# Attention with global tokens and an expert layer: q and k transposed on TensorE, or cast through DRAM and transposed by DMA

## The chip, the cores and the metric

The kernel runs on one core of one Trainium2 chip. The metric is the device time of one execution in microseconds (us). Executions of one kernel mostly agree within about 0.5%. "Faster" or "slower" needs a difference of 2% that is clear of noise.

Engines: PE is TensorE's matmul, PEld its weight load, DVE is VectorE, ACT is ScalarE, POOL is GpSimd, SP is SyncE. On this kernel SP only issues DMAs. POOL also casts, and its DMAs go through another queue than SP's.

## The reference, cut to what matters

There are 8 batches of 8 heads. Each head has 512 local and 32 global tokens of 64 elements. Local tokens attend to the globals and to local tokens within a distance of 32; globals attend to all.

```python
k_all = concat([k_g, k_l]); v_all = concat([v_g, v_l])
out_g = softmax(scale * q_g @ k_all.T) @ v_all
s_l   = concat([scale * q_l @ k_g.T, where(|i-j| <= 32, scale * q_l @ k_l.T, -1e9)])
out_l = softmax(s_l) @ v_all
x = concat([out_g, out_l]) as (4352 tokens, 512)
h = x @ w_in                       # 512 -> 2048
out = (h * clip(h + 3, 0, 6) / 6) @ w_out
```

## The kernel before

The work of a batch is four pairs of heads. The kernel's score matmuls take q and k with the 64 elements of each head on the partitions: `kT` and `qT`, 128 partitions for two heads. DRAM holds them token by token. From the third batch on the kernel before does this:

```python
# SP loads q and k as fp32, tokens on the partitions        (load_qk)
nc.sync.dma_start(out=nat[b][0][i][:, kb], in_=(k_l, q_l)[i][b, :, kb*P:(kb+1)*P, :].rearrange(...))
# POOL casts a pair's part to fp16                           (cast_rows)
copies[i](out=r[m][i], in_=f[i][:, :, 2*m:2*m+2])

def emit_globals(b):               # once a batch: 8 matmuls, one DVE cast, two ACT casts
    ...
    nc.tensor.matmul(out=gT[:, i, m], lhsT=gz[b % 2][:, i, 2*m:2*m+2]..., rhs=ident[:, 0:Sg])
    nc.vector.tensor_copy(out=kgT[b % 2], in_=gT[:, 0])
    for e in range(2):
        nc.scalar.copy(out=qgz[b % 2][r, :, e*Sg:(e+1)*Sg], in_=gT[r, 1])

def emit_T(p):                     # once a pair: 8 transposes, 4 DVE copies, 1 ACT copy
    psT = ps_tile("psT", FP16)     # one of 7 PSUM buffers that everything shares
    for t, ps in zip(nat[b][1][m], src):
        for j in range(NT):
            nc.tensor.matmul(out=ps[:, j*P:(j+1)*P], lhsT=t[:, j]..., rhs=ident, is_transpose=True)
    nc.vector.tensor_copy(out=kT[:, <two places for the globals>], in_=kgT[b % 2][:, m:m+1]...)
    for k0, k1, c0 in SEG:         # three segments
        nc.vector.tensor_copy(out=kT[:, c0:c0 + k1 - k0], in_=src[0][:, k0:k1])
    nc.scalar.copy(out=qT, in_=src[1])

def emit_QK(p):                    # scores: psG for the globals, four psS buffers
    ...
    for t in range(2):
        pss = [ps_tile(f"psS{e}") for e in range(2)]
        ...                        # psS matmuls of this half
        for e in range(2):
            nc.scalar.activation(out=E[:, e, t], in_=pss[e][:, 0:SW], func=EXP, scale=qk_scale)
            nc.vector.tensor_tensor(out=E[:, e, t], in0=E[:, e, t], in1=mask[:, t], op=mult)
        ...

for p in range(NPAIR):             # software pipeline over pairs
    ...
    emit_T(p + 2)
    cast_rows(b + 1, m, pool)
    M(1)                           # M(n): n units of the previous batch's expert layer
    emit_QK(p + 1)
    M(4)
    emit_AV(p, lambda: M(1))
    M(2)
```

A unit of M is four 128x512 matmuls, into `psH` (first layer; ACT and DVE then make `t` and `gt` of it) or into `po` (second layer; DVE copies it to `ot`). The order on PE, ACT and DVE is set by a scheduler that starts from this program order; the order on POOL and SP is that of the program.

The softmax here doesn't subtract the row's maximum and nothing guards it: scores larger than these inputs give would overflow.

Of the kernel before, what the change touches and what calls it, by code (L numbers as in the profile page):

```python
# [9 lines left out]
FP32 = mybir.dt.float32  # L10
FP16 = mybir.dt.float16
# [3 lines left out]
def kernel(  # L15
# [12 lines left out]
    nc = tc.nc  # L28
    ctx.enter_context(tc.manual_schedule(engines={mybir.EngineType.Pool, mybir.EngineType.SP}))
    P = 128  # L30
    B, H, Sl, D = q_l.shape
    Sg = q_g.shape[2]
    S = Sg + Sl
    dm, dff = moe_w_in.shape
    NM = H // 2
    NC = dff // P
    NT = Sl // P
# [9 lines left out]
    SEG = [(0, 128, 0), (128, 288, 160), (288, 512, 352)]  # L47
    KC = [0, 128, 192, 320, 448]
    GC = [128, 320]
    KW = Sl + 2 * Sg  # L50
# [14 lines left out]
    natp = ctx.enter_context(tc.tile_pool(name="natp", bufs=2))  # L65
    wrk = ctx.enter_context(tc.tile_pool(name="wrk", bufs=2))
    moew = ctx.enter_context(tc.tile_pool(name="moew", bufs=4))
    psp = ctx.enter_context(tc.tile_pool(name="psp", bufs=7, space=bass.MemoryType.PSUM))
    psg = ctx.enter_context(tc.tile_pool(name="psg", bufs=1, space=bass.MemoryType.PSUM))

    def ps_tile(name, dtype=FP32):
        return psp.tile([P, 2048 // (4 if dtype == FP32 else 2)], dtype, tag="ps", name=name)
# [3 lines left out]
    def const(name, shape, dtype=FP16):  # L76
        return constp.tile(shape, dtype, tag=name, name=name)

    ident = const("ident", [P, P])
    kgT = [const(f"kgT{i}", [P, NM, Sg]) for i in range(2)]  # L80
# [10 lines left out]



    NR = 2

    def f_rows(t):
        return t.rearrange("p (kb h d) -> p kb h d", kb=NT, h=H)

    def load_runs(b, i, h0, nh):
        nc.gpsimd.dma_start(  # L100
# [8 lines left out]

    nat = {}  # L110

    def new_nat(b):
        if b < NR:
            f = [natp.tile([P, H, NT, D], FP16, tag=t, name=t, bufs=1) for t in ("k16", "q16")]
        else:
            f = [f_rows(natp.tile([P, NT * H * D], FP32, tag=t, name=t, bufs=1))
                 for t in ("f0", "f1")]
        nat[b] = (f, {})

    def load_qk(b):  # L120
        new_nat(b)
        for i in range(2):
            if b < NR:
                load_runs(b, i, 0, H)
                continue
            for kb in range(NT):
                nc.sync.dma_start(
                    out=nat[b][0][i][:, kb],
                    in_=(k_l, q_l)[i][b, :, kb * P:(kb + 1) * P, :].rearrange("h s d -> s h d"))


    def load_g(b, t=None):
        for i, src in enumerate((k_g, q_g)):
            (nc.gpsimd if t is None else nc.sync).dma_start(
                out=gz[b % 2][0:Sg, i] if t is None else t[:, i],
                in_=src[b].rearrange("h s d -> s h d"))

    def cast_rows(b, m, copies):
        f, r = nat[b]
        r[m] = [natp.tile([P, NT, 2, D], FP16, tag=f"{t}{m}", name=f"{t}{m}") for t in ("kr", "qr")]  # L140
        for i in range(2):
            copies[i](out=r[m][i],
                      in_=(f[i][:, 2 * m:2 * m + 2].rearrange("p h j d -> p j h d")
                           if b < NR else f[i][:, :, 2 * m:2 * m + 2]))

    def load_v(b):
        for c, r0, r1, src in v_parts(b, 0, H):
# [8 lines left out]
    def load_vf(b, h0, nh):  # L156
        for c, r0, r1, src in v_parts(b, h0, nh):
            nc.sync.dma_start(out=vf[b][r0:r1, c, h0:h0 + nh], in_=src)
# [4 lines left out]

    first = (nc.vector.tensor_copy, nc.scalar.copy)
    pool = (nc.gpsimd.tensor_copy, nc.gpsimd.tensor_copy)
    new_nat(0)
    new_vf(0)
    for i in range(2):
        load_runs(0, i, 0, 2)
# [33 lines left out]
    def emit_globals(b):  # L203
        psT = ps_tile("psGT")
        gT = psT[:, 0:2 * NM * Sg].rearrange("d (i m s) -> d i m s", i=2, m=NM)
        for i in range(2):
            for m in range(NM):
                nc.tensor.matmul(out=gT[:, i, m],
                                 lhsT=gz[b % 2][:, i, 2 * m:2 * m + 2].rearrange("s h d -> s (h d)"),
                                 rhs=ident[:, 0:Sg])  # L210
        nc.vector.tensor_copy(out=kgT[b % 2], in_=gT[:, 0])
        for e in range(2):
            r = slice(e * D, (e + 1) * D)
            nc.scalar.copy(out=qgz[b % 2][r, :, e * Sg:(e + 1) * Sg], in_=gT[r, 1])

    st = {}

    def emit_T(p):
        b, m = divmod(p, NM)
        kT = wrk.tile([P, KW], FP16, tag="kT", name="kT", bufs=4)  # L220
        qT = wrk.tile([P, Sl], FP16, tag="qT", name="qT", bufs=4)
        if b < NR:
            src = [ps_tile("psT") for _ in range(2)]
        else:
            psT = ps_tile("psT", FP16)
            src = [psT[:, i * Sl:(i + 1) * Sl] for i in range(2)]
        for t, ps in zip(nat[b][1][m], src):
            for j in range(NT):
                lhs = t[:, j].rearrange("p h d -> p (h d)")
                if b < NR:  # L230
                    nc.tensor.matmul(out=ps.rearrange("d (p j) -> d j p", j=NT)[:, j],
                                     lhsT=lhs, rhs=ident)
                else:
                    nc.tensor.matmul(out=ps[:, j * P:(j + 1) * P], lhsT=lhs, rhs=ident,  # L234
                                     is_transpose=True)
        nc.vector.tensor_copy(
            out=kT[:, GC[0]:GC[0] + 2 * (GC[1] - GC[0])].rearrange("d (i s) -> d i s", i=2)[:, :, 0:Sg],
            in_=kgT[b % 2][:, m:m + 1].to_broadcast([P, 2, Sg]))
        for k0, k1, c0 in SEG:
            nc.vector.tensor_copy(out=kT[:, c0:c0 + k1 - k0], in_=src[0][:, k0:k1])  # L240
        nc.scalar.copy(out=qT, in_=src[1])  # L241
        st[p] = dict(qT=qT, kT=kT)

    def emit_QK(p):
        b, m = divmod(p, NM)
        s = st[p]
        qT, kT = s["qT"], s["kT"]
        E = wrk.tile([P, 2, 2, SW], FP16, tag="E", name="E", bufs=3)
        Eg = wrk.tile([P, NCH, 2 * Sg], FP16, tag="Eg", name="Eg", bufs=3)
        s["E"], s["Eg"] = E, Eg  # L250
        psG = ps_tile("psG")
        for c in range(NCH):
            nc.tensor.matmul(out=psG[:, c * 2 * Sg:(c + 1) * 2 * Sg],  # L253
                             lhsT=kT[:, KC[c]:KC[c] + P], rhs=qgz[b % 2][:, m])
        for t in range(2):
            pss = [ps_tile(f"psS{e}") for e in range(2)]
            for c in range(NCH):
                if SC[c][0] != t:
                    continue
                c0, (_, _, q0, nq) = SC[c][1], CH[c]  # L260
                for e in range(2):
                    r = slice(e * D, (e + 1) * D)
                    nc.tensor.matmul(out=pss[e][:, c0:c0 + nq], lhsT=kT[r, KC[c]:KC[c] + P],  # L263
                                     rhs=qT[r, q0:q0 + nq])
            if t == 0:
                nc.scalar.activation(out=Eg, in_=psG[:, 0:NCH * 2 * Sg], func=EXP, scale=qk_scale)  # L266
# [3 lines that stand above are left out]
            if t == 0:  # L270
                nc.vector.tensor_tensor(out=Eg[:, 2:4], in0=Eg[:, 2:4], in1=maskg, op=mult)
# [116 lines left out]
    cast_vf(0, 3)  # L388
    new_vf(1)
    load_vf(1, 0, H)  # L390
    nc.vector.memset(vn[1][:, :, :, D:P], 1.0)
    for i in range(NC // 4):
        load_w_out(i)
# [4 lines left out]
    for p in range(NPAIR):  # L398
        b, m = divmod(p, NM)
        if m == 0 and b >= 1 and b + 1 < B:  # L400
            load_g(b + 1)
            load_v(b + 1)
        if p == NM:
            M(2)
            emit_globals(1)
            emit_T(p)
            M(1)
            emit_T(p + 1)
            M(1)
            emit_QK(p)  # L410
            M(1)
            load_qk(2)
        if m == 2 and 1 <= b < B - 1:
            emit_globals(b + 1)
        if p + 2 < NPAIR and p not in (NM - 2, NM - 1):
            emit_T(p + 2)
        if 1 <= b < B - 1:
            cast_rows(b + 1, m, pool)
            if m == NM - 1 and b + 2 < B:
                load_qk(b + 2)  # L420
        M(1)
        if p + 1 < NPAIR and p != NM - 1:
            emit_QK(p + 1)
        M(4)
        emit_AV(p, lambda: M(1))
        if m == NM - 1:
            M(len(units))
            units += moe_units(
                lambda mm, b=b: xts[b][mm], Sl,
                [[(0, P, b * S + Sg + t * P)] for t in range(NT)])  # L430
        else:
            M(2)
# [35 lines left out]
```

## Time and profile before

368.63 us, median of 3 runs (367.38 to 369.09).

| reading | before |
|---|---|
| span of the profiled execution | 366.0 us |
| PE busy | 91% |
| DVE, ACT busy | 68%, 68% |
| one batch in the steady part | 39.73 us |

The page's parts 1 and 2: busy time of PE, then the span in 40 slices, each digit the busy share of its slice in tenths.

```profile
span 366.0 us, 6783 instructions
...
PE 332.0 (91%) x2560; PEld 184.6 (50%) x2560; DVE 248.1 (68%) x577; ACT 247.0 (68%) x477; POOL 92.0 (25%) x144
...
PE   2575799998999999999999999999999999999994
...
ACT  2597399559975698559964897569855995274070
...
DMA  9999999259404990099107920397001000100202
...
```

PE is nearly full from the sixth slice on. ACT swings between nearly full (attention with the expert first layer) and half empty (with the second layer). The DMA row has zeros and ones in a good part of the steady slices. So there is idle DMA time to which work could be moved.

The windows view gives the steady state. The edges are the starts of the `xg` operations on DVE (the first of two a batch), which end each batch's attention. Columns: window, its length, then busy us and number of instructions of each engine.

```profile
...
core 0: us, PE busy (x) PEld busy (x) DVE busy (x) ACT busy (x) POOL busy (x), PEclk, DMA share, GB/s
123.91:163.64 39.73, 38.43 (x308) 20.82 (x308) 28.31 (x67) 29.53 (x57) 11.00 (x18) 1.00 0.60 93
163.64:203.38 39.74, 38.44 (x308) 20.86 (x308) 28.35 (x68) 29.52 (x57) 11.12 (x18) 1.00 0.68 104
...
```

What the transposes cost on PE, and how PE waits afterwards, is in the timeline of PE, in one pair of the fourth batch (start, duration, line, operation, count; in brackets idle time and who ended it):

```profile
...
132.69 0.39 PE L234 MATMUL psT<-ident,kr_1697 128*128 128x128 f16 x4
132.91 0.39 PE L234 MATMUL psT<-ident,qr_1698 128*128 128x128 f16 x4
...
134.81 0.29 PE L263 MATMUL psS_2037<-qT,kT 64*128 64x320 f16 x1 [0.19 <-DVE gt L330]
135.41 0.29 PE L263 MATMUL psS_2038<-qT,kT 64*128 64x320 f16 x1 [0.31 <-DVE gt L330]
...
```

Four transposes start every 0.22 us, so a pair's eight take 0.44 us of the stream, though each is shown with a longer duration (they are pipelined). The later psS matmuls wait twice for a PSUM buffer that DVE must empty. The timeline of ACT at the same place:

```profile
...
135.10 0.57 ACT L268 ACTIVATE E<-psS_2023 128x480 f16<-128x480 f32 x1
135.85 0.59 ACT L241 COPY qT<-psT 128x512 f16<-128x512 f16 x1 [0.18 <-DVE kT L240]
136.34 0.58 ACT L268 ACTIVATE E<-psS_2024 128x480 f16<-128x480 f32 x1
...
```

The qT copy stands between the first and the second E. It takes 0.49 us of ACT's stream, after 0.18 us of idle time in which it waits for DVE, and so puts off the three E operations that empty psS.

### The profile page before, as it was taken

The numbers are of one execution on the slowest core, as the hardware profiler recorded it, in microseconds if no ns is written. First come the engines' busy times: TensorE is split into PE (matmuls) and PEld (weight loads), VectorE is DVE, ScalarE is ACT, GpSimd is POOL, SyncE is SP. The second block draws the span as 40 slices with busy tenths as digits, with TensorE's granted clock in tenths as the row PEclk, the third lists the DMA queues.
The fourth block names the chain that finished last, engine by engine and source line by source line (L and its number), as shares of the span: only waits on it lengthen the run. The fifth ranks groups of instructions, "written<-read, shape, count | busy, mean of one in ns | idle before, by whom it ended". The sixth has DMA issues, their size and how long they took to land.

```text
span 366.0 us, 6783 instructions
## 1 busy us (share of the span) xinstructions
PE 332.0 (91%) x2560; PEld 184.6 (50%) x2560; DVE 248.1 (68%) x577; ACT 247.0 (68%) x477; POOL 92.0 (25%) x144
## 2 busy tenths in 40 slices
PE   2575799998999999999999999999999999999994
PEld 1553455565455555555555545555555544544471
DVE  7774698558875588558855888558855884485171
ACT  2597399559975698559964897569855995274070
POOL 7561581507400650044300830064000000000000
PEclk9996699999999999999999999999999999999998
DMA  9999999259404990099107920397001000100202
GB/s 149 214 196 184 200 210 160 36 140 211 47 3 111 206 107 2 29 201 189 9 31 152 226 18 2 108 209 102 3 30 57 30 1 30 57 30 0 86 31 57
DMA packets 109713, 35.38 MB, mean 97 GB/s; under 512 B 97136, under 2 KB 105328, under 8 KB 109680
## 3 DMA queue, kind: packets, MB, share of 16 engines
q0 software_dynamic: 43648, 10.69, 30.0%
q1 hardware_dynamic: 66032, 24.26, 29.9%
q8 instruction: 20, 0.33, 0.4%
q14 instruction: 13, 0.11, 0.1%
HBM read 36.70 MB, written 8.91 MB: 125 GB/s over the span
## 4 chain that ended last, share of the span: by engine, by line
PE 43%; ACT 29%; DVE 12%; DMA 7%; issue 5%; POOL 2%; DVEq 0%; ACTq 0%; POOLq 0%
PE po L339 28%; PE psH L324 7%; ACT E L268 7%; ACT Ln L300 5%; DMA gz_82<-in_q_g_dram 5%; DVE gt L330 4%; PE pav L296 4%; ACT Rc L303 3%; ACT qT L241 2%; DMA q_98<-in_q_l_dram 2%; DVE kT L240 1%; PE psT L234 1%; PE pg L298 1%; ACT Eg L266 1%; ACT Lg L311 1%
## 5 line engine op out<-in xcount | busy, mean ns | idle before, releaser
L339 PEld LDWEIGHTS <-gt 128*128 128x128 f16 x544 | 49.5, 97 | 54.1 <-issue 2.5
L300 ACT ACTIVATE Ln<-pav 64x512 f32<-64x512 f32 x64 | 38.0, 593 | 42.1 <-PE pav L296 36.4
L269 DVE TENSOR_TENSOR E<-E,mask 128x480 f16<-128x480 f16 x128 | 50.6, 410 | 9.6 <-ACT E L268 6.6
L343 DVE COPY ot<-po 128x512 f32<-128x512 f32 x34 | 23.5, 691 | 25.4 <-PE po L339 24.4
L339 PE MATMUL po<-wout_93,gt 128*128 128x512 f16 x136 | 35.0, 379 | 0.0
L339 PE MATMUL po<-wout_92,gt 128*128 128x512 f16 x136 | 34.9, 379 | 0.0
L339 PE MATMUL po<-wout_95,gt 128*128 128x512 f16 x136 | 34.9, 379 | 0.0
L339 PE MATMUL po<-wout_94,gt 128*128 128x512 f16 x136 | 34.9, 378 | 0.0
L148 POOL DMA_DIRECT2D vn_87<-in_v_l_dram x15 | 12.6, 850 | 67.6 <-PE pg L298 53.5
L148 POOL DMA_DIRECT2D vn_86<-in_v_l_dram x15 | 12.8, 864 | 49.0 <-PE pg L298 49.0
L266 ACT ACTIVATE Eg<-psG 128x320 f16<-128x320 f32 x32 | 13.9, 436 | 15.0 <-PE psG L253 14.9
L296 PE MATMUL pav<-E,vn_86 128*128 128x160 f16 (+3 forms) x160 | 21.5, 251 | 2.2 <-ACT Eg L266 1.2
L263 PEld LDWEIGHTS <-kT 64*128 64x128 f16 x320 | 12.8, 95 | 18.1 <-issue 13.8
L296 PE MATMUL pav<-E,vn_87 128*128 128x160 f16 (+3 forms) x160 | 21.3, 244 | 0.0
L324 PEld LDWEIGHTS <-win_88 128*128 128x128 f16 x144 | 14.0, 103 | 13.3 <-issue 2.0
L303 ACT ACTIVATE Rc<-Ln 128x512 f32<-128x512 f32 x32 | 20.0, 626 | 0.7
L324 PEld LDWEIGHTS <-win_90 128*128 128x128 f16 x144 | 13.3, 98 | 13.1 <-issue 1.2
L324 PEld LDWEIGHTS <-win_89 128*128 128x128 f16 x144 | 13.2, 98 | 12.5 <-issue 0.6
L324 PEld LDWEIGHTS <-win_91 128*128 128x128 f16 x144 | 13.1, 98 | 12.2 <-issue 0.2
L296 PEld LDWEIGHTS <-vn_86 128*128 128x128 f16 x160 | 14.9, 99 | 7.4 <-issue 3.1
L298 PE MATMUL pg<-Eg,vn_87 128*128 128x32 f16 x160 | 18.6, 178 | 0.0
L296 PEld LDWEIGHTS <-vn_87 128*128 128x128 f16 x160 | 14.9, 97 | 5.2
(967 smaller groups left out, 847.8 us busy)
## 6 DMA issues: line engine op xcount, KB each, us to landing
out_dram<-ot SPq DMA_DIRECT2D x32, 256.0 KB, 2.1
vn_86<-in_v_l_dram POOLq DMA_DIRECT2D x9, 128.0 KB, 6.8
vn_87<-in_v_l_dram POOLq DMA_DIRECT2D x9, 128.0 KB, 6.2
f_679<-in_k_l_dram SPq DMA_DIRECT2D x4, 256.0 KB, 5.8
f_680<-in_q_l_dram SPq DMA_DIRECT2D x4, 256.0 KB, 7.9
f_1135<-in_k_l_dram SPq DMA_DIRECT2D x4, 256.0 KB, 4.3
f_1136<-in_q_l_dram SPq DMA_DIRECT2D x4, 256.0 KB, 5.6
f_1701<-in_k_l_dram SPq DMA_DIRECT2D x4, 256.0 KB, 4.4
```

What stands on the lines that cost most here:

```text
L148: nc.gpsimd.dma_start(out=vn[b % NV][r0:r1, c, :, 0:D], in_=src)
L266: nc.scalar.activation(out=Eg, in_=psG[:, 0:NCH * 2 * Sg], func=EXP, scale=qk_scale)
L268: nc.scalar.activation(out=E[:, e, t], in_=pss[e][:, 0:SW], func=EXP, scale=qk_scale)
L269: nc.vector.tensor_tensor(out=E[:, e, t], in0=E[:, e, t], in1=mask[:, t], op=mult)
L296: nc.tensor.matmul(out=pav[:, q0:q0 + nq], lhsT=lhs, rhs=E[:, e, t, c0:c0 + nq], start=(i == 0), stop=(i == NCH - 1), skip_group_check=True)
L298: nc.tensor.matmul(out=pg[:, m, e], lhsT=lhs, rhs=Eg[:, c, e * Sg:(e + 1) * Sg], start=(i == 0), stop=(i == NCH - 1), skip_group_check=True)
L300: nc.scalar.activation(out=Ln[e * D:(e + 1) * D], in_=pav[D:P, 0:Sl], func=LN)
L303: nc.scalar.activation(out=Rc, in_=Ln, func=EXP, scale=-1.0)
L324: nc.tensor.matmul(out=ps[:, 0:n], lhsT=w_in_t[c // 4][:, m, (c % 4) * P:(c % 4 + 1) * P], rhs=rhs(m), start=(m == 0), stop=(m == NM - 1))
L330: nc.vector.scalar_tensor_tensor(out=gts[c][:, 0:n], in0=t1[:, 0:n], scalar=1.0, in1=ps[:, 0:n], op0=amin, op1=mult)
L339: nc.tensor.matmul(out=po[t][:, 0:dm], lhsT=gts[c][:, t * P:(t + 1) * P], rhs=w_out_t[c // 4][:, c % 4], start=(c == 0), stop=(c == NC - 1))
L343: nc.vector.tensor_copy(out=ot, in_=po[t][:, 0:dm])
```

## The change

The intent is to take the transposes, their copies and the POOL casts out of the compute engines. From the third batch on POOL issues DMAs that cast q and k from fp32 to fp16 into a DRAM buffer, token by token, with the global rows already in their places. SP then issues DMA transposes from there straight into `kTb` and `qTb`. The rows of `qgz` that must be zero are written into that buffer once. Core of the diff:

```diff
+    scr = [dramp.tile([2, KW, H, D], FP16, tag=f"scr{i}", name=f"scr{i}") for i in range(2)]
+    def cast_qk(b):
+        t = scr[b % 2]
+        def put(i, r0, src):
+            nc.gpsimd.dma_start(out=t[i, r0:r0 + src.shape[1]], in_=src.rearrange("h s d -> s h d"))
+        for k0, k1, c0 in SEG:
+            put(0, c0, k_l[b, :, k0:k1])
+        for c in GC:
+            put(0, c, k_g[b])
+        put(1, 0, q_l[b])
+        ...                                       # q_g, every other head
+    def transpose_qk(b):
+        tr[b] = [natp.tile([P, NM, KW], FP16, tag=t, name=t) for t in ("kTb", "qTb")]
+        for m in range(NM):
+            for i in range(2):
+                nc.sync.dma_start_transpose(
+                    out=tr[b][i][:, m], in_=scr[b % 2][i, :, 2*m:2*m+2].rearrange("s h d -> s (h d)"))
     def emit_T(p):
         b, m = divmod(p, NM)
+        if b >= NR:                               # NR = 2
+            k, q = tr[b]
+            st[p] = dict(kT=k[:, m], qT=q[:, m, 0:Sl], qg=q[:, m, Sl:KW])
+            return
         ...
         if m == 0 and b >= 1 and b + 1 < B:
-            load_g(b + 1)
+            if b + 1 > NR:
+                cast_qk(b + 1)
             load_v(b + 1)
         ...
-            load_qk(2)
+            cast_qk(NR)
         if m == 2 and 1 <= b < B - 1:
-            emit_globals(b + 1)
+            transpose_qk(b + 1)
         ...
-        if 1 <= b < B - 1:
-            cast_rows(b + 1, m, pool)
-            if m == NM - 1 and b + 2 < B:
-                load_qk(b + 2)
```

More of the change, by code (lines that the diff above doesn't have):

```diff
@@ L68 @@
     psp = ctx.enter_context(tc.tile_pool(name="psp", bufs=7, space=bass.MemoryType.PSUM))
+    dramp = ctx.enter_context(tc.tile_pool(name="dramp", bufs=1, space=bass.MemoryType.DRAM))
     psg = ctx.enter_context(tc.tile_pool(name="psg", bufs=1, space=bass.MemoryType.PSUM))
@@ L94, with zero_scr @@
     NR = 2
-    def f_rows(t):
-        return t.rearrange("p (kb h d) -> p kb h d", kb=NT, h=H)
+    scr = [dramp.tile([2, KW, H, D], FP16, tag=f"scr{i}", name=f"scr{i}") for i in range(2)]
+    zero = const("zero", [Sg, NM, D])
+    def zero_scr():
+        nc.vector.memset(zero, 0.0)
+        for t in scr:
+            for e in range(2):
+                nc.sync.dma_start(
+                    out=t[1, Sl + e * Sg:Sl + (e + 1) * Sg].rearrange("s (m e) d -> e s m d", e=2)[1 - e],
+                    in_=zero)
+    def cast_qk(b):
+        t = scr[b % 2]
+        def put(i, r0, src):
+            nc.gpsimd.dma_start(out=t[i, r0:r0 + src.shape[1]],
+                                in_=src.rearrange("h s d -> s h d"))
+        for k0, k1, c0 in SEG:
[3 more added lines that the diff above has]
+        put(1, 0, q_l[b])
+        for e in range(2):
+            nc.gpsimd.dma_start(
+                out=t[1, Sl + e * Sg:Sl + (e + 1) * Sg].rearrange("s (m e) d -> e s m d", e=2)[e],
+                in_=q_g[b].rearrange("(m e) s d -> e s m d", e=2)[e])
+    tr = {}
+    def transpose_qk(b):
[3 more added lines that the diff above has]
+                nc.sync.dma_start_transpose(
+                    out=tr[b][i][:, m], in_=scr[b % 2][i, :, 2 * m:2 * m + 2].rearrange("s h d -> s (h d)"))
     def load_runs(b, i, h0, nh):
@@ L110 @@
     nat = {}
-    def new_nat(b):
-        if b < NR:
-            f = [natp.tile([P, H, NT, D], FP16, tag=t, name=t, bufs=1) for t in ("k16", "q16")]
-        else:
-            f = [f_rows(natp.tile([P, NT * H * D], FP32, tag=t, name=t, bufs=1))
-                 for t in ("f0", "f1")]
-        nat[b] = (f, {})
     def load_qk(b):
-        new_nat(b)
-        for i in range(2):
-            if b < NR:
+        nat[b] = ([natp.tile([P, H, NT, D], FP16, tag=t, name=t, bufs=1) for t in ("k16", "q16")],
+                  {})
+        if b:
+            for i in range(2):
                 load_runs(b, i, 0, H)
-                continue
-            for kb in range(NT):
-                nc.sync.dma_start(
-                    out=nat[b][0][i][:, kb],
-                    in_=(k_l, q_l)[i][b, :, kb * P:(kb + 1) * P, :].rearrange("h s d -> s h d"))
     def load_g(b, t=None):
@@ L134, in load_g @@
             (nc.gpsimd if t is None else nc.sync).dma_start(
-                out=gz[b % 2][0:Sg, i] if t is None else t[:, i],
+                out=gz[b][0:Sg, i] if t is None else t[:, i],
                 in_=src[b].rearrange("h s d -> s h d"))
@@ L142, in cast_rows @@
             copies[i](out=r[m][i],
-                      in_=(f[i][:, 2 * m:2 * m + 2].rearrange("p h j d -> p j h d")
-                           if b < NR else f[i][:, :, 2 * m:2 * m + 2]))
+                      in_=f[i][:, 2 * m:2 * m + 2].rearrange("p h j d -> p j h d"))
     def load_v(b):
@@ L165 @@
     pool = (nc.gpsimd.tensor_copy, nc.gpsimd.tensor_copy)
-    new_nat(0)
+    load_qk(0)
     new_vf(0)
@@ L208, in emit_globals @@
                 nc.tensor.matmul(out=gT[:, i, m],
-                                 lhsT=gz[b % 2][:, i, 2 * m:2 * m + 2].rearrange("s h d -> s (h d)"),
+                                 lhsT=gz[b][:, i, 2 * m:2 * m + 2].rearrange("s h d -> s (h d)"),
                                  rhs=ident[:, 0:Sg])
-        nc.vector.tensor_copy(out=kgT[b % 2], in_=gT[:, 0])
+        nc.vector.tensor_copy(out=kgT[b], in_=gT[:, 0])
         for e in range(2):
             r = slice(e * D, (e + 1) * D)
-            nc.scalar.copy(out=qgz[b % 2][r, :, e * Sg:(e + 1) * Sg], in_=gT[r, 1])
+            nc.scalar.copy(out=qgz[b][r, :, e * Sg:(e + 1) * Sg], in_=gT[r, 1])
     st = {}
@@ L219, in emit_T @@
         b, m = divmod(p, NM)
+        if b >= NR:
+            k, q = tr[b]
+            st[p] = dict(kT=k[:, m], qT=q[:, m, 0:Sl], qg=q[:, m, Sl:KW])
+            return
         kT = wrk.tile([P, KW], FP16, tag="kT", name="kT", bufs=4)
         qT = wrk.tile([P, Sl], FP16, tag="qT", name="qT", bufs=4)
-        if b < NR:
-            src = [ps_tile("psT") for _ in range(2)]
-        else:
-            psT = ps_tile("psT", FP16)
-            src = [psT[:, i * Sl:(i + 1) * Sl] for i in range(2)]
+        src = [ps_tile("psT") for _ in range(2)]
         for t, ps in zip(nat[b][1][m], src):
             for j in range(NT):
-                lhs = t[:, j].rearrange("p h d -> p (h d)")
-                if b < NR:
-                    nc.tensor.matmul(out=ps.rearrange("d (p j) -> d j p", j=NT)[:, j],
-                                     lhsT=lhs, rhs=ident)
-                else:
-                    nc.tensor.matmul(out=ps[:, j * P:(j + 1) * P], lhsT=lhs, rhs=ident,
-                                     is_transpose=True)
+                nc.tensor.matmul(out=ps.rearrange("d (p j) -> d j p", j=NT)[:, j],
+                                 lhsT=t[:, j].rearrange("p h d -> p (h d)"), rhs=ident)
         nc.vector.tensor_copy(
             out=kT[:, GC[0]:GC[0] + 2 * (GC[1] - GC[0])].rearrange("d (i s) -> d i s", i=2)[:, :, 0:Sg],
-            in_=kgT[b % 2][:, m:m + 1].to_broadcast([P, 2, Sg]))
+            in_=kgT[b][:, m:m + 1].to_broadcast([P, 2, Sg]))
         for k0, k1, c0 in SEG:
@@ L241, in emit_T @@
         nc.scalar.copy(out=qT, in_=src[1])
-        st[p] = dict(qT=qT, kT=kT)
+        st[p] = dict(qT=qT, kT=kT, qg=qgz[b][:, m])
     def emit_QK(p):
@@ L253, in emit_QK @@
             nc.tensor.matmul(out=psG[:, c * 2 * Sg:(c + 1) * 2 * Sg],
-                             lhsT=kT[:, KC[c]:KC[c] + P], rhs=qgz[b % 2][:, m])
+                             lhsT=kT[:, KC[c]:KC[c] + P], rhs=s["qg"])
         for t in range(2):
@@ L390 @@
     load_vf(1, 0, H)
+    zero_scr()
     nc.vector.memset(vn[1][:, :, :, D:P], 1.0)
```

## The prediction

> What bounds the kernel now. The page gives PE 91% busy over the 366.0 us span, DVE 68%, ACT 68%, POOL 25%. From about 66 us on, one batch takes 39.7 us (the chain of waits: po stretches start at 106.2, 145.9, 185.7 us), of which the table by windows has PE busy 38.7 of 40 at full clock. TensorE is the bound, ScalarE close behind in attention (9.4 of 10 us in 130-140). In the timeline a pair of heads spends 0.44 us on eight 128x128 transposes (x4 in 0.22 us) and loses roughly 0.6 to 1.0 us in gaps before the later psS matmuls for PSUM that DVE (gt, ot) and ACT must empty. Summing issue steps, a batch is about 36.2 us of matmul stream (my estimate) and 3.5 us of such gaps.
>
> What the change removes, for 24 pairs (batches 2 to 7): 192 transposes and 48 global matmuls on PE: 4 x 0.44 + 0.2 = 1.95 us a batch. On ACT four qT copies (586 ns alone, about 0.48 us in the full stream) and two qgz casts (0.26): about 2.4 us a batch. On DVE four times three kT copies (230 ns) and the global-column copy, and one kgT cast (0.28): about 3.6 us. On POOL eight casts of 0.62 us a batch. One PSUM allocation of about 14 in each pair goes too.
>
> Critical: all of the PE part. ACT shrinks as much, so it is no new limit. The copies also sit ahead of the gt and E work that frees PSUM; I expect 0.3 to 0.7 us a batch less of gaps. Together 2.4 us a batch, six batches: about 14 us. A batch then takes 37.3 us.
>
> What it adds: DMA work only. Per batch about 9,000 cast packets (256 B read, 128 B written to DRAM) in place of 8,192 plain loads, and eight transposes of 147 KB. In 240 to 251 us about 10,200 packets went through in 11 us, 17 ns a packet on each of 16 engines. At that rate (estimates) the casts take 10 us, twice that if small DRAM writes are slow; the v loads 6; output 2.5. For the transposes, the Trainium skill ("DMA: Bandwidth & Descriptors", Latency and other measured facts) states 261 GB/s with a non-contiguous middle dimension: about 4.5 us a batch; I allow up to 12. No run here shows it yet. Sum 23 to 40 us of a 37 us batch, centre 29: it fits. Latency is hidden: POOL issued the v loads of batch 2 at 48 us, so its casts start near 53 us, the transposes can start near 68 us (after the first output on SP), and the first kT is needed near 95 us. Later batches have some 30 us.
>
> Prediction: 355.5 us, range 349 to 369. Faster by over 2%: 0.75; within: 0.14; slower: 0.11.
>
> What would show it: the period of the po stretches falls to 37 to 37.7 us; batches 0 and 1 (to about 66 us) unchanged; no PE or weight-load wait on the transposes' DMA in the list of waits; gaps before psS shorter but present; DMA busy in most slices; ACT in the attention stretches under 9 of 10 us.
>
> What would make it wrong: transposes or 128 B DRAM writes several times dearer than taken, so that DMA exceeds a batch and QK waits on kTb or qTb (then 370 to 400 us); transposes on SP delaying outputs until ot buffers run out; PSUM gaps that only move, so that PE's gain is given back as waits for ACT or DVE (then 359 to 363); or gaps that shrink more than thought (349 to 352).

## More of the kernel before

A batch is 39.73 us, of which PE is busy 38.43. PE is idle for 1.30 us, DVE for 11.4 and ACT for 10.2.

## The result, and the profile after

The changed kernel takes 352.86 us (median of 4 runs, 352.26 to 354.01); the kernel before took 368.23 us in the 4 runs that it is compared with. The ratio is 0.9586, with a 95% interval of 0.9549 to 0.9624: faster. A ratio here is the mean time of one kernel's fast runs over that of the other's of the same rounds, so not quite the ratio of the medians. All outputs are right.

The same parts of the page, after:

```profile
span 350.3 us, 6244 instructions
...
PE 318.1 (91%) x2320; PEld 172.0 (49%) x2320; DVE 230.1 (66%) x476; ACT 232.1 (66%) x441; POOL 101.7 (29%) x132
...
PE   2595599998999999999999999999999999999994
...
ACT  2598299549984699359954896489746992472160
...
DMA  8999999999991899249971999199011000100102
...
```

The digits of PE look the same, the span is shorter. The DMA row has filled up, with short pauses in each batch. The steady state in the windows view, same edges and columns:

```profile
...
119.92:157.03 37.11, 36.09 (x268) 18.75 (x268) 25.16 (x50) 27.05 (x52) 12.63 (x16) 1.00 1.12 110
...
231.25:268.37 37.12, 36.09 (x268) 18.77 (x268) 25.17 (x51) 27.07 (x52) 2.61 (x4) 1.00 0.52 75
...
```

A batch is 37.11 us, 2.62 less. PE is busy 2.34 us less, ACT 2.48, DVE 3.15. PE's idle time has shrunk by only 0.28 us, to 1.02. The second row tells one thing already: that window has no casts any more, only the last batch's eight transposes (DMA share 0.52 in place of 1.12; the column adds up overlapping packets, so it can exceed 1), and it lasts just as long. The casts of the other batches cost them nothing.

Where the 15.7 us between the two spans lie, from the xg starts: 1.65 up to the end of the second batch, which already has half of the third batch's transposes; 2.34 in the third; 4 x 2.62 in the next four; 1.2 after that, where the last two pairs' transposes were. So nearly the whole gain is in the batches that the change touches. (A little of the 1.65 may be the clock: between 41.4 and 60 us the windows view shows a granted clock of 0.98 after and 0.96 before, some 0.4 us by my estimate from these two.)

The gap in the score matmuls is still there, in the timeline of PE:

```profile
...
138.30 0.31 PE L272 MATMUL psG<-qTb,kTb 128*128 128x64 f16 x5
138.54 0.59 PE L282 MATMUL psS<-qTb,kTb 64*128 64x160 f16 x7
139.54 0.36 PE L282 MATMUL psS<-qTb,kTb 64*128 64x320 f16 x3 [0.41 <-DVE gt L349]
...
```

One wait of 0.41 us for DVE remains in this pair. Over the whole batch the timeline lists four waits of PE before the change, all at psS (0.36, 0.19, 0.31 and 0.23 us, 1.1 together), and three after it: two at psS (0.41 each) and one of 0.21 at psH. So the waits at psS are fewer but not each shorter, and the sum of all waits has hardly fallen.

The DMA view (operation, count, size, median us from issue to landing) tells what the new work takes:

```profile
...
scr<-in_q_l_dram POOLq DMA_DIRECT2D x6, 512.0 KB, 14.4
...
kTb<-scr SPq DMA_TRANSPOSE x24, 6.5
qTb<-scr SPq DMA_TRANSPOSE x24, 6.9
...
```

The medians hide a range: the eight transposes of the fourth to seventh batch, with casts beside them, land after 7.2 to 8.0 us in the median, those of the eighth, with none, after 3.7.

And the timeline of SP and of PE at the first use, by the third batch's first pair:

```profile
...
67.55 0.38 SPq L364 DMA_DIRECT2D out_dram<-ot  x1
68.16 1.50 SPq L133 DMA_TRANSPOSE kTb<-scr  x1
69.89 1.13 SPq L133 DMA_TRANSPOSE qTb<-scr  x1
...
```

```profile
...
75.82 1.46 PE L358 MATMUL po<-wout,gt 128*128 128x512 f16 x6
77.11 0.31 PE L272 MATMUL psG<-qTb,kTb 128*128 128x64 f16 x5
...
```

SP is occupied for 1.1 to 2.5 us by the issue of one transpose (0.38 for an output of 256 KB). The first pair's two were issued at 68.16 and 69.89 us, and PE used them at 77.11 without a wait. They had landed at 74.77 and 75.31, so that first use had 1.8 us to spare; the next batch's transposes are issued from 82.10 us on and first used at 110.71. The list of waits has no wait of PE for kTb or qTb.

### The profile page after: what moved, and what is told of

It reads as the page before. It is cut to its first block, busy times and chain, and to the rows that moved or that the text cites. A ratio compares the mean times of both kernels' runs of the same rounds, so it can differ in the third digit from the quotient of the medians.

```text
span 350.3 us, 6244 instructions
## 1 busy us (share of the span) xinstructions
PE 318.1 (91%) x2320; PEld 172.0 (49%) x2320; DVE 230.1 (66%) x476; ACT 232.1 (66%) x441; POOL 101.7 (29%) x132
## 4 chain that ended last, share of the span: by engine, by line
PE 57%; ACT 16%; DVE 9%; DMA 7%; issue 5%; POOL 2%; SPq 1%; DVEq 0%; POOLq 0%; ACTq 0%
PE po L358 30%; PE psH L343 18%; ACT t L347 7%; DVE xt L325 7%; DMA gz<-in_q_g_dram 6%; PE pav L315 5%; ACT Ln L319 4%; ACT Rc L322 3%; DVE gt L349 3%; PE psS L282 3%; ACT E L287 2%; SPq L182 1%; DMA vf<-in_v_g_dram 1%; PE pg L317 1%; PE psT L253 1%
## 5 line engine op out<-in xcount | busy, mean ns | idle before, releaser
L358 PE MATMUL po<-wout,gt 128*128 128x512 f16 x544 | 125.6, 379 | 0.0
L343 PE MATMUL psH<-xt,win 128*128 128x512 f16 x512 | 121.4, 381 | 1.6 <-DVE xt L325 1.0
L347 ACT ACTIVATE t<-psH,half_col 128x512 f32<-128x512 f32 (+1 forms) x144 | 90.5, 678 | 22.0 <-PE psH L343 20.2
L349 DVE SCALAR_TENSOR_TENSOR gt<-t,psH 128x512 f16<-128x512 f32 (+1 forms) x144 | 90.9, 660 | 13.8 <-ACT t L347 11.7
L343 PEld LDWEIGHTS <-win 128*128 128x128 f16 x576 | 53.5, 98 | 53.5 <-issue 3.7
L325 DVE TENSOR_TENSOR xt<-Rc,pav 64x512 f16<-64x512 f32 x64 | 43.6, 681 | 52.7 <-ACT Rc L322 51.7
L287 ACT ACTIVATE E<-psS 128x480 f16<-128x480 f32 x128 | 62.8, 589 | 0.0
L315 PE MATMUL pav<-E,vn 128*128 128x160 f16 (+3 forms) x320 | 44.1, 251 | 1.8 <-ACT Eg L285 1.0
L315 PEld LDWEIGHTS <-vn 128*128 128x128 f16 x320 | 30.6, 100 | 12.7 <-issue 2.5
L317 PE MATMUL pg<-Eg,vn 128*128 128x32 f16 x320 | 36.5, 179 | 0.0
L317 PEld LDWEIGHTS <-vn 128*128 128x128 f16 x320 | 27.4, 96 | 7.1 <-issue 0.8
## 6 DMA issues: line engine op xcount, KB each, us to landing
scr<-in_q_l_dram POOLq DMA_DIRECT2D x6, 512.0 KB, 14.4
```

Source lines behind the costliest of these rows:

```text
L315: nc.tensor.matmul(out=pav[:, q0:q0 + nq], lhsT=lhs, rhs=E[:, e, t, c0:c0 + nq], start=(i == 0), stop=(i == NCH - 1), skip_group_check=True)
L317: nc.tensor.matmul(out=pg[:, m, e], lhsT=lhs, rhs=Eg[:, c, e * Sg:(e + 1) * Sg], start=(i == 0), stop=(i == NCH - 1), skip_group_check=True)
L325: nc.vector.tensor_tensor(out=xts[b][m][r], in0=Rc[r], in1=pavs[e][0:D, 0:Sl], op=mult)
L343: nc.tensor.matmul(out=ps[:, 0:n], lhsT=w_in_t[c // 4][:, m, (c % 4) * P:(c % 4 + 1) * P], rhs=rhs(m), start=(m == 0), stop=(m == NM - 1))
L347: nc.scalar.activation(out=t1[:, 0:n], in_=ps[:, 0:n], func=RELU, bias=half_col, scale=1.0 / 6.0)
L349: nc.vector.scalar_tensor_tensor(out=gts[c][:, 0:n], in0=t1[:, 0:n], scalar=1.0, in1=ps[:, 0:n], op0=amin, op1=mult)
```

## The experiments

My theory after the result was: in the steady part PE's stream is the bound, the transposes were in it, and the copies and casts on ACT and DVE cost little except where they delay the emptying of PSUM. The rival: the gain comes mainly from the copies. A second question was whether the DMA work is free, and how much room is left. Three more runs ask whether the gaps that remain can be filled, and whether the change can be extended.

### Putting work back: transposes, copies, globals

Each run takes the changed kernel and adds unread work to the 24 pairs.

```diff
# e1_pe_back, in emit_T for b >= NR
+            psT = ps_tile("psT", FP16)
+            for i in range(2):
+                for j in range(NT):
+                    nc.tensor.matmul(out=psT[:, i*Sl + j*P:i*Sl + (j+1)*P], lhsT=ident, rhs=ident, is_transpose=True)
# e2_pe_copies_back: that, and the copies of before from psT into unread kTd, qTd
+            nc.vector.tensor_copy(out=kTd[:, <globals>], in_=kgT[b % 2]...)
+            for k0, k1, c0 in SEG:
+                nc.vector.tensor_copy(out=kTd[:, c0:c0 + k1 - k0], in_=psT[:, k0:k1])
+            nc.scalar.copy(out=qTd, in_=psT[:, Sl:2*Sl])
# e3_copies_only: no PE work, no PSUM tile; sources that lie in SBUF from the start
+                nc.vector.tensor_tensor(out=kTd[:, c0:c0 + k1 - k0], in0=base[...], in1=base[...], op=mult)
+            nc.scalar.copy(out=qTd, in_=w_in_t[0][:, 0])
# e4_globals_back, beside transpose_qk(b + 1)
+            emit_globals((b + 1) % 2)
```

> The changed kernel plus, for each of the 24 pairs of batches 2 to 7, eight 128x128 PE transposes of the identity into a PSUM tile that nobody reads; no copies. Theory A (the PE stream is the bound, so 0.44 us of transposes in a pair is 0.44 us of time): 24 x 0.44 = 10.6 us back, about 363.4 us. Rival B (the gain came from the ACT and DVE copies that no longer stand ahead of the work that frees PSUM): at most 3 us back, under 356 us.

> As the run before, and the PSUM tile is copied out as in the kernel before: four DVE copies to a kT that nobody reads, one ACT copy to a qT that nobody reads. Theory A: 363 to 365 us, hardly more than with the transposes alone. Rival B: most of the 15.4 us comes only here, 362 to 366 us while the run before stays under 356. From the 0.62 us that the kernel before lost with the last batch's globals I expect 2.0 us a batch here, 12 us, 365 us.

> The changed kernel plus the copies alone, from SBUF and unread: a 128x512 ACT copy and four DVE operations in each of the 24 pairs, nothing on PE and no PSUM tile. Theory A: under 2 us back (below 355), as ACT and DVE have 10 us free in a batch of 37.1. Rival B: 6 to 12 us back.

> The changed kernel plus the eight global matmuls, the kgT cast and two qgz casts once in each of batches 2 to 7, unread. If only PE's stream counts: 6 x 0.2 = 1.2 us back, 354.1. If the step between the kernel before's 39.73 us batches and its last of 39.11, which had no globals to make, is their price: 6 x 0.62 = 3.7 us, 356.6.

Measured: 360.19 us with the transposes (ratio to before 0.9779), 365.51 with transposes and copies (0.9924), 358.17 with the copies alone (0.9718), 353.47 with the globals (0.9595). The transposes alone fall between theory A and the rival, 363.4 and under 356.

The third of these is a miss of construction. Nothing held those copies in their pair, since their sources were ready from the start. The trace has 110 of the 120 on DVE and ACT between 60 and 86 us (all between 56 and 95), where they pushed PE's work back by some 6 us; the batches after that were 37.12 us again. It says nothing of the steady state. The repair takes E of two pairs before as the source, which keeps each copy near its pair:

```diff
# e3b_copies_in_place
+            Es = st[p - 2]["E"][:, 0].rearrange("p t w -> p (t w)")
+            for k0, k1, c0 in SEG:
+                nc.vector.tensor_tensor(out=kTd[:, c0:c0 + k1 - k0], in0=Es[:, 0:k1-k0], in1=Es[:, 256:256 + k1-k0], op=mult)
+            nc.scalar.copy(out=qTd, in_=Es[:, 0:Sl])
# e8_all_back: e2 and e4 together
```

> The copies alone once more, but with E of two pairs before as their source, so that they stay in their pair (in the first try nothing held them and they were all done between 60 and 86 us, so that run says nothing of the steady state). In steady state (37.11 us a batch after the change, 38.33 with the transposes alone back, 39.15 with both): if a copy only costs when it delays the emptying of PSUM that PE waits for, the period rises by 0.3 to 0.8 us, 354.5 to 358 us in all. If PE alone sets the period: under 0.2 us, below 354.5.

> The changed kernel with all removed work on PE, ACT and DVE put back unread (transposes, copies, globals), so that only the way in which q and k come differs from the kernel before. If the 15.4 us came from that work, the period is 39.7 us again and the time 366 to 369 us. If a part of the gain came from elsewhere (POOL casts, fewer plain loads), it stays at or below 365.5.

Measured: 356.80 us (0.9687) with the copies in their pairs, where the DVE operations take 232 ns and the ACT copy 618 ns in the median (231 and 587 in the run that copies from PSUM). And 368.37 us (1.0007, interval 0.9966 to 1.0048) with everything back: the kernel before's time, though q and k still come by DMA transposes.

The windows view, one batch of each run: transposes, transposes and copies, copies, everything.

```profile
...
121.80:160.12 38.32, 37.65 (x300) 20.57 (x300) 25.73 (x50) 27.09 (x51) 12.60 (x16) 1.00 1.10 106
...
```

```profile
...
123.17:162.31 39.14, 38.01 (x300) 20.62 (x300) 27.81 (x66) 29.02 (x55) 12.62 (x16) 1.00 1.08 104
...
```

```profile
...
121.40:159.20 37.80, 36.36 (x268) 18.85 (x268) 27.05 (x67) 29.22 (x56) 12.64 (x16) 1.00 1.14 108
...
```

```profile
...
125.03:164.76 39.73, 38.43 (x308) 20.84 (x308) 28.12 (x68) 29.52 (x57) 12.63 (x16) 1.00 1.07 103
...
```

The last row has PE busy 38.43 us in 39.73, the very numbers of the kernel before. Its timeline also has the same four waits of PE at psS, to within 0.01 us. So the whole gain is the work taken off PE, ACT and DVE, with the PSUM buffers that it held; POOL's casts and the plain loads gave nothing that shows. The parts of it, as the mean period of four batches in the steady part:

| changed kernel plus | period, us | against 37.11 |
|---|---|---|
| nothing | 37.11 | |
| globals | 37.14 | +0.03 |
| copies in their pairs | 37.80 | +0.69 |
| transposes | 38.33 | +1.22 |
| transposes and copies | 39.15 | +2.04 |
| transposes, copies, globals | 39.74 | +2.63 |
| the kernel before | 39.73 | +2.62 |

Two things follow. First, both theories have a part: PE work is the larger one, but the copies cost between a quarter and a third of the gain (0.69 alone, 0.82 on top of the transposes). The transposes cost 1.22 alone and 39.15 - 37.80 = 1.35 on top of the copies. Their stream time is 4 x 0.44 = 1.76 us a batch: PE's idle time falls from 1.02 to 0.67 us when they are put back alone, so some of the work is done in gaps that were there anyway. PE's timeline in that batch shows which. The two waits of 0.41 us at psS and the one of 0.21 at psH are gone, and these two are all that it has in their place:

```profile
...
123.15 3.61 PE L348 MATMUL psH<-xt,win 128*128 128x512 f16 x16 [0.29 <-DVE ot L367]
...
132.97 3.61 PE L348 MATMUL psH<-xt,win 128*128 128x512 f16 x16 [0.23 <-DVE gt L354]
...
```

Second, the parts depend on what is there already. The globals cost 0.03 us alone and 0.59 on top of the rest. The three parts measured singly add up to 1.94 us, so singly they miss a quarter of the 2.63 that they are worth together. Why the globals cost so much more on top of the rest is not shown. Nor do these runs separate a part's operations from the PSUM buffer that it takes: the runs with transposes hold a `psT`, and with the copies put back as well it stays taken until they have read it. Only the copies in their pairs are free of this.

### Doubling the DMA work

```diff
# e5_transposes_twice: after the eight transposes, eight more into a tile that nobody reads
+                nc.sync.dma_start_transpose(out=xx[i][:, m], in_=scr[b % 2][i, :, 2*m:2*m+2]...)
# e6_casts_twice, e9_casts_three_times
-        t = scr[b % 2]
+        for t in (scr[b % 2], scx[b % 2]):                    # e6
+        for t in (scr[b % 2], scx[b % 2], scx[2 + b % 2]):    # e9
+            cast_one(b, t)
```

> Each batch's eight DMA transposes done a second time into a tile that nobody reads, right after the first eight. If the DMA work of the change is hidden with room to spare: within 0.5 us of 352.9. If it sits near its limit: QK starts to wait for kTb or qTb and the time rises by several us.

> Each batch's casts into DRAM done twice, the second into a buffer that nobody reads; the transposes wait for the first only. In the trace of the changed kernel the queues work some 24 of the 37 us of a batch, of which I put 14 to 16 on the casts: doubled, 38 to 40 of 37 us, so here the limit should show: the period becomes 38 to 42 us, 356 to 378 us. If the DMA has more room than that reading says: within 1 us of 352.9.

> Each batch's casts into DRAM done three times, two of them unread. With the casts twice the queues worked in 98% of a 37.11 us batch, without loss, one set of casts costing about 12 us: three sets need 48 us. So here QK, and AV for its v, must wait: about 11 us a batch from batch 3 on, 385 to 410 us. If not, the busy share of the queues is no measure of their limit, and it stays under 360.

Measured: transposes twice 352.92 us (0.9586); casts twice 354.76 (0.9628, interval 0.9588 to 0.9667, which overlaps the changed kernel's); casts three times 370.57 in a single look, of unknown state. One batch of the first two in the windows view, and of the second the DMA row of that window:

```profile
...
119.89:157.00 37.11, 36.08 (x268) 18.77 (x268) 25.14 (x50) 27.06 (x52) 12.63 (x16) 1.00 1.42 146
...
```

```profile
...
121.47:158.58 37.11, 36.09 (x268) 18.76 (x268) 25.14 (x50) 27.05 (x52) 23.82 (x28) 1.00 2.00 167
...
```

```profile
...
DMA  9999999999999999999999999999999999999999
...
```

With the casts twice every slice of the DMA row is full, and the batch still lasts 37.11 us. My expectation of a limit there was a miss. It took "some queue is busy in this slice" for "the queues are used up". The Trainium skill ("Perfetto Trace Analysis", Identifying the Most-Contended Engine) says that 16 engines make the occupancy of DMA misleading. The loss of that run lies before the steady part. At the first use PE waits 0.60 us for the transposes and starts the scores at 78.66 us in place of 77.11:

```profile
...
78.66 0.31 PE L276 MATMUL psG<-qTb,kTb 128*128 128x64 f16 x5 [0.60 <-DMA qTb<-scr]
...
```

The other 0.95 us were lost before that wait: 0.32 by the end of the first batch, and some 0.4, by my estimate, to a granted clock of 0.96 in place of 0.98 between 41 and 60 us. The rest I have not traced.

With the casts three times the limit shows, later and smaller than I expected: batches of 41.04, 40.76, 40.53 and 38.01 us, and 40.73 for the next one. Not all of it is waiting: in four of these five the granted clock is 0.96 in place of 1.00, and in the first of them PE is busy for 37.92 us in place of 36.09 and idle for 3.12 in place of 1.02. It shows in another place as well, in the list of waits (who waited for whom, us in total, times, longest):

```profile
...
PE pav L319 <- DMA vn<-in_v_l_dram: 9.7, 8, 2.8
...
```

In the steady part PE waits for v and not for kTb (its one wait for qTb, 1.2 us, is at the first use). The v loads stand behind the casts in POOL's program order, and POOL itself waits up to 7.2 us for casts to land before it issues the next. So the added work of the change had the room of one more whole set of casts a batch, and, by this single look, less than two. Whether DMA bandwidth or POOL's order of issue is what ran out is not separated.

### Extending the change to the second batch

```diff
# e10_from_batch_1
-    NR = 2
+    NR = 1
-    load_qk(1); load_g(1)
+    cast_qk(1)
     zero_scr()
+    transpose_qk(1)
-        cast_rows(1, m, pool)
-            emit_globals(1)
```

> The change applied from the second batch on (batch 1 too is cast in DRAM and transposed by DMA; the change itself starts with the third). Removes four more pairs' transposes and copies, the batch's globals and POOL casts: up to 2.6 us less. But these casts must pass in the start-up, in which the queues are full until about 60 us and PE waits for them until 39 us: a detour through DRAM there delays batch 1's first QK. I expect 352 to 360 us, so no gain; under 351 would say that the start-up is no obstacle.

Measured: 360.19 us (0.9774), 7.3 more than the change. The steady period is 37.10 us (the change's 37.11), so the loss is in the start. The list of waits shows it:

```profile
...
PE psG L272 <- DMA qTb<-scr: 13.9, 2, 13.1
...
```

PE waits 13.1 us for one transpose. In the start-up the DMA queues are full with weights, v and the first batches' q and k, and the detour through DRAM makes the batch's first scores late. The expectation of no gain was right; the time is just beyond the upper end of its range.

### Filling the gap that remains

```diff
# e7_qk_split, on the changed kernel; e11_before_split, the same on the kernel before
-    def emit_QK(p):
+    def emit_QK(p, mid=lambda: None):
         ...
             if t == 0:
                 nc.vector.tensor_tensor(out=Eg[:, 2:4], in0=Eg[:, 2:4], in1=maskg, op=mult)
+                mid()
         ...
-            emit_QK(p + 1)
-        M(4)
+            emit_QK(p + 1, lambda: M(1))
+            M(3)
+        else:
+            M(4)
```

> The changed kernel with one unit of expert matmuls (0.865 us) moved between the two halves of each pair's psS matmuls, to fill the gap in which PE waits there for a PSUM buffer. About 2.9 us of a 37.11 us batch are such gaps (PE issue steps sum to 34.2, an estimate). If they can be filled by order alone: 1 to 2 us a batch less, 342 to 347 us. If ACT and DVE set the pace of emptying PSUM whatever the order: 352 to 354 us, as the gap only moves.

> The kernel before, with PE transposes and all copies, with only the reordering that took the changed kernel from 352.9 to 348.7 us (a unit of expert matmuls between the two halves of the psS matmuls). If the change and the reordering remove different time, the reordering saves about the same 4 us here: 363 to 365 us. If part of what the change saved was the same PSUM gap, which the reordering can also fill (the copies' part of the change, 0.8 of 2.6 us a batch), it saves more here: 357 to 362 us. If ACT sets the pace here, nothing: 367 to 369.

Measured on the changed kernel: 348.66 us (0.9457, interval 0.9427 to 0.9488), the best of all. The timeline of PE in one pair, and a batch in the windows view:

```profile
...
129.00 0.31 PE L272 MATMUL psG<-qTb,kTb 128*128 128x64 f16 x5
129.24 0.38 PE L282 MATMUL psS<-qTb,kTb 64*128 64x160 f16 x6
129.56 1.04 PE L344 MATMUL psH<-xt,win 128*128 128x512 f16 x4
130.53 0.38 PE L282 MATMUL psS<-qTb,kTb 64*128 64x320 f16 x4
...
```

```profile
...
119.95:156.35 36.40, 36.19 (x268) 18.24 (x268) 25.22 (x50) 27.15 (x52) 12.63 (x16) 1.00 1.22 112
...
```

The wait between the two halves of psS is gone: a unit of psH runs there. PE is idle for 0.21 us of a batch, where the changed kernel had 1.02. The period is 36.41 us on average, 0.70 less: 2.8 us in the four steady batches, and another 0.9 after them. That is less than the 1 to 2 us a batch that I expected, but not nothing.

On the kernel before the same edit gives 365.69 us (0.9931, inside 2%, though its interval, 0.9902 to 0.9960, excludes 1). One batch:

```profile
...
122.98:162.58 39.60, 38.59 (x308) 20.38 (x308) 28.23 (x68) 29.39 (x57) 10.99 (x18) 1.00 0.61 94
...
```

Here the period only falls from 39.73 to 39.60 us and PE keeps 1.01 us of idle time. Of the 2.3 us between the two spans 0.9 lie before the third batch's end, 0.5 in the four steady batches and 0.9 after them. None of the three expectations fits well. The total is near the first, the steady part is near the last. So the reordering is worth 0.70 us a batch after the change and 0.13 without it. What keeps PE's gap open before the change is not shown. My reading was the copies, which stand in ACT's and DVE's way. A rival is the PSUM that the copies read: in one pair of this run `psGT` and `psT` are written from 141.41 us on and read out only from 144.47 on, and PE's wait of 0.47 us for a buffer ends between the two, at 144.01. So two of the seven buffers are held across that wait, and the copies come after it. No run took the copies or those buffers alone out of the kernel before.

## Why the prediction was right, and where it was off

The measured 352.86 us lies in the range of 349 to 369, and the forecast of faster (0.75) came true. The gain was put at 13.1 us and was 15.4.

- **The period.** Predicted 37.3 us a batch, with 37 to 37.7 as the sign; measured 37.11. The saving of 2.62 us was put at 2.4.
- **PE's removed work is all critical.** Off as an attribution. The transposes are worth 1.22 us alone and 1.35 on top of the copies, of their 1.76, and the globals alone 0.03. The sum of 1.95 and "0.3 to 0.7 less of gaps" is near 2.62, but it is not made in that way: transposes 1.22, copies on top of them 0.82, globals on top of both 0.59. PE's part was put too high, and the copies and globals too low. That these two errors nearly cancel is luck; that the removed work on PE, ACT and DVE is the whole gain, as predicted, is shown.
- **The gaps before psS.** Less in sum but present, as said: the waits at psS come to 0.82 us a batch in place of 1.1. PE's whole idle time fell by 0.28 us, just under the 0.3 to 0.7 that I gave. (By the sums of issue steps, which are estimates, the gaps fell from 3.5 to 2.9 us.)
- **ACT under 9 of 10 us in attention.** Wrong. In two 10 us windows of the changed kernel's attention (120 to 140 us) it is 9.55 and 9.51. ACT does 2.48 us less in a batch, but the attention part has become shorter with it. A busy share does not show work removed where the stretch shrinks as well; busy time in a whole batch does.
- **DMA fits.** Right: no wait of PE for the transposes, and both doublings free in the steady state. I had put the sum at 23 to 40 us of a batch, as the cost of small writes into DRAM was unknown. The DMA row of a steady batch after the change adds up to some 23 us (an estimate from its digits), the low end of that. The 4.5 us for the transposes in it was an estimate from the skill's rate, which no run tests.
- **Times of issue.** The casts began at 50.9 us (predicted 53), the transposes at 68.16 (68). But the first use was at 77.11 us and not near 95: I had misread where in the second batch the next one's first scores are placed. With the transposes landing 2.8 to 6.6 us after issue there it still held, though with 1.8 us to spare, and not in the run with doubled casts. This part was luck.
- **Latency in later batches.** 28.6 us between the first issue (82.10) and the first use (110.71) in the fourth batch, where I said 30.

## What to carry to other kernels

Where TensorE is the full engine and the DMA queues have idle time, as here, layout work can go to the queues even though a single DMA transpose takes far longer than one on TensorE (medians of 3.7 to 8.0 us to landing against 0.44 us for a pair's eight); ask whether its latency is hidden and whether the queues are free at that point of the program, and leave the start-up alone. Measure a part's worth by putting it back in its place in the finished kernel, singly and together, as parts need not add up; check in the trace that the scheduler left it there. After such a change look at the order again: a gap that the new order hardly closed before (0.13 us a batch here) may now close (0.70).

## What the Trainium skill lacked or had wrong

- "VectorE: DVE Perf Modes", The three transpose paths and its rules: it gives 390 ns for a 128x128 transpose on TensorE and 1309 ns on the DMA crossbar, and advises TensorE if a PSUM destination is acceptable. Here eight in a row start every 54 ns on PE (0.22 us for four), and a DMA transpose of 576x128 landed 6.5 to 6.9 us after its issue in the median over the run. Yet the DMA path saved 2.62 us a batch, because PE was the bound and the PSUM result had to be copied out as well. The advice lacks the copies and the question of which engine is full.
- "DMA: Bandwidth & Descriptors", Latency and other measured facts: it states 261 GB/s for DMA transposes with a non-contiguous middle dimension. No run here reaches or tests that rate, as the issue comes first: SP took about 1.27 us to issue one of 576x128 in fp16 (147 KB), so eight took 12 us. No page gives this issue time for trn2 and this size by name; the nearest figure on that page is for small tiles of earlier chips that it does not name.
- No page has the cost of a casting DMA from DRAM to DRAM. Here 512 KB (after the cast) landed 14.4 us after issue in the median, and two whole sets of a batch's casts (1 MB each) fitted into 37.11 us beside everything else; three did not, in a single look.
- "Perfetto Trace Analysis", Identifying the Most-Contended Engine, is right that DMA occupancy misleads: all 40 slices of a batch at 90% or more, and no loss. The page's remark on consistent bubbles, under Optimization Strategy, (they can mean too little PSUM or SBUF) is only half of it here: the same gap in two pairs of every batch went away by order alone, with the same seven buffers, PE's idle time falling from 1.02 to 0.21 us a batch.
